# Decay attention and a snake MLP on one core: masks written directly in bf16, and the order of all engines written anew

## The chip, the core and the metric

The kernel runs on one NeuronCore of a Trainium2 chip. Its engines are TensorE (PE, its weight loads PEld), VectorE (DVE), ScalarE (ACT), GpSimd (POOL) and SyncE (SP); an issue queue is written with a q (SPq, POOLq). The metric is the device time of one execution in microseconds (us). A measurement is the median of several executions.

## What is computed

Causal attention with a decay per head, over 4 batches, 8 heads, 768 positions and head dimension 64, and behind it a two-layer MLP on the 3072 tokens of width 512 with 2048 hidden units:

```python
for b in range(nb):                      # blocks of 64 positions, in order
    intra = np.einsum('bhic,bhjc->bhij', qb, kb) * Dmask[None]      # lam**(i-j), i >= j
    intra = np.einsum('bhij,bhjd->bhid', intra, vb)
    inter = np.einsum('bhid,bhde->bhie', qb * lam_pow[None], kv_state)
    out[:, :, sl] = intra + inter
    kv_state = lam_block[None, :, None, None] * kv_state + np.einsum('bhsd,bhse->bhde', kb_dec, vb)
x = np.ascontiguousarray(attn_out.transpose(0, 2, 1, 3)).reshape(B * S, H * D)
h = x @ w_in
s = np.sin(alpha * h)
g = h + s * s / (alpha + 1e-09)
return (g @ w_out).astype(np.float32)
```

## The kernel before

**Attention.** The kernel takes blocks of 128 positions: 24 of them, six a batch. The decay is put into the operands: q is multiplied by lam to the position (L471 for the first four blocks, L481 for later ones), k by lam to minus the position (L488, L500). The factors `Lq`, `Lk`, `Lp` are Exp on ACT (L446 to L452) of `lnL`, a VectorE product (L444) of `E_f` and the logarithm of lam (L441); `E_f` is a GpSimd cast (L420) of three IOTA (L414, L416, L418). What remains of the decay mask is a mask of ones and zeros. v is only cast to bf16 (L494, L503). A block's q and k are transposed (on TensorE for the first eight blocks, L542, L569 and L519, by DMA later, L509) and copied out of PSUM as `qkT` (L547, L580, L552, L524). Then S, all scores of a block (L621), goes to PSUM; VectorE multiplies it by the mask and writes `Sm` in bf16 (L632); Z adds the block's k and v to the running state in PSUM bank 7 (L657, L665), which is copied out as `Zd` or `Zc` (L675, L681); and O adds Sm times v (L768 for the first four blocks, L725 later) and the state times q (L788, L703, L716). The result is cast to bf16 as `xT` (L748, L735), the transposed input of the MLP.

**MLP.** It takes six chunks of 512 tokens (four blocks). Stage A makes 16 products of 128 hidden units: L831 with 512 columns at once, L865 with two halves of 256. Each goes to one PSUM bank; ACT takes Sin of it (`t`, L841 or L875), ACT or GpSimd squares that (`u`, L845/L846 or L879/L880), and VectorE forms `gT` (L848, L883) from u and the bank, which is free again then. Stage B multiplies by w_out: directly for chunk 0 (L896); for the others by Strassen's scheme of seven products (L984), for which sums of weights (L939, into `ws`, `Ta` and `w`) and of tokens (L962, `Xs` and `gT`) are made on VectorE or GpSimd, and VectorE combines the results (L1024, L1030). Attention of later blocks stands between the products of earlier chunks.

**Loads.** SP issues the loads of q, k and v in its order; each waits until its ring buffer is free. The first 512 columns of w_in come in f32 as `ws` and are cast (L395). The other three blocks of w_in and the four of w_out come as DMAs that GpSimd issues (L326); they wait for the first v, and the loads of blocks 4 and 5 of q and behind it wait for the w_in block of columns 1024 to 1535 (the second of the three).

**The masks.** There are three: masks 0 and 1 for the first four blocks, whose positions are interleaved, mask 2 for all others. VectorE sets all three to one in f32 (`maskf`, L427), GpSimd clears what lies ahead of the diagonal (L431: two instructions of 64 rows each for masks 0 and 1, one of 128 rows for mask 2), and VectorE casts each to bf16 (L436).

**The order.** Each operation is recorded with an index, in program order (`op`). `ORDER` holds, for each engine, the list of the indices that it runs, in this order; where an operation may run on one of several engines, the list that holds it decides. A pair like `(31, 512)` in TensorE's list is filler: 31 products of the constant tile `idle` (a part of `Xs`) with 512 columns, whose result nobody reads (L1143). `_settle` walks the lists, and `emit` puts the waits in front of each instruction (L431's instructions on masks 0 and 1 wait for the GpSimd instruction ahead of them).

Of the kernel before, what the change touches and what calls it, by code (L numbers as in the profile page):

```python
# [8 lines left out]
F32 = mybir.dt.float32  # L9
# [26 lines left out]
class _Plan:  # L36
# [16 lines left out]
        ),  # L53
        "ACT": (
# [162 lines left out]
def bass_lightning_attn__then__act_snake_kernel(  # L217
# [41 lines left out]
    with es:  # L259

        def sb(name, shape, dt):
            return es.enter_context(nc.sbuf_tensor(name, shape, dt))
# [29 lines left out]
        mask = ring("mask", 3, [128, 128], BF16)  # L292
        maskf = sb("maskf", [128, 3, 128], F32)
# [21 lines left out]
        def _(_unused_eng):  # L315
# [4 lines left out]
            op = P.op  # L320
# [107 lines left out]
            for i in range(3):  # L428
                t, ks = (4, 2) if i < 2 else (2, 1)
# [828 lines left out]
```

## Time and profile before

| | |
|---|---|
| median of 3 runs | 212.16 us (211.62 to 213.02) |
| profiled execution | 212.84 us |
| its span, from the first to the last instruction | 211.0 us |
| busy share of the span | PE 95%, DVE 79%, ACT 72%, PEld 64%, POOL 61% |
| HBM read, written | 27.28 MB, 6.29 MB |

The profile is of one execution. The page gives busy time by engine, the timeline gives one row for each run of like instructions on an engine: start and length in us, engine, line, operation, what it writes and reads, count, and in brackets how long the engine had been idle and what ended that. The chain of waits follows the end of the program back, at each step to what released it. A busy TensorE includes matmuls that overlap: one of 512 columns shows as 379 ns, while they follow each other more closely.

### The profile page before, as it was taken

How to read it: one execution, taken by the hardware profiler on the slowest of the kernel's cores; microseconds unless marked ns; L12 is line 12 of the kernel's file. 1: busy time of each engine (PE TensorE's matmuls, PEld its weight loads, DVE VectorE, ACT ScalarE, POOL GpSimd, SP SyncE). 2: the span in 40 equal slices, each digit the busy share in tenths (PEclk: the TensorE clock that was granted, in tenths of full speed). 3: DMA queues.
4: the chain of work that ended last, by engine and by line, in shares of the span. 5: the costliest groups of instructions: out<-in, count | busy, mean ns of one | idle time of the engine just before them, and what ended most of it. 6: DMA issues, size and time to landing. Idle time of an engine off the chain costs nothing.

```text
span 211.0 us, 4818 instructions
## 1 busy us (share of the span) xinstructions
PE 201.1 (95%) x1927; PEld 135.5 (64%) x1950; DVE 167.5 (79%) x295; ACT 152.7 (72%) x279; POOL 127.9 (61%) x133
## 2 busy tenths in 40 slices
PE   6998899989999999999999999999999999999995
PEld 2476544546777787666566577666667666676994
DVE  1788467886779999989999988789886787587833
ACT  4448887837999999996777886976996667767100
POOL 5123476957698784955693653864995464923620
PEclk9999999999999999999999999999999999999999
DMA  4999999999969999997999998248000000500424
GB/s 135 313 314 224 211 225 196 252 198 254 260 120 180 226 201 249 228 241 190 209 224 197 236 204 234 42 109 243 3 0 0 3 0 0 199 3 0 168 71 163
DMA packets 83222, 34.40 MB, mean 163 GB/s; under 512 B 59632, under 2 KB 80384, under 8 KB 83200
## 3 DMA queue, kind: packets, MB, share of 16 engines
q1 hardware_dynamic: 78544, 29.24, 62.2%
q0 software_dynamic: 3696, 3.67, 10.8%
q10 hardware_dynamic: 960, 1.19, 1.9%
q8 instruction: 15, 0.25, 0.5%
q14 instruction: 7, 0.06, 0.1%
HBM read 27.28 MB, written 6.29 MB: 159 GB/s over the span
## 4 chain that ended last, share of the span: by engine, by line
PE 69%; DVE 16%; ACT 11%; issue 2%; ACTq 0%
PE bank L831 25%; PE bank L984 22%; PE bank L896 5%; PE bank L865 5%; PE bank L1143 5%; DVE gT L883 4%; ACT u L845 3%; DVE Sm L632 3%; ACT t L841 3%; DVE gT L848 3%; PE bank L621 2%; PE bank L725 2%; ACT Zd L675 1%; DVE Xs L962 1%; PE bank L657 1%
## 5 line engine op out<-in xcount | busy, mean ns | idle before, releaser
L831 PE MATMUL bank<-xT,w 128*128 128x512 bf16 x279 | 67.6, 379 | 2.8 <-issue 0.6
L848 DVE SCALAR_TENSOR_TENSOR gT<-u,rinv,bank 128x512 bf16<-128x512 bf16 x74 | 53.8, 742 | 17.6 <-ACT u L845 11.7
L841 ACT ACTIVATE t<-bank,alpha 128x512 bf16<-128x512 f32 x74 | 49.9, 683 | 21.4 <-PE bank L831 20.7
L831 PEld LDWEIGHTS bank<-xT,w 128*128 128x128 bf16 x296 | 27.6, 98 | 29.3 <-DVE gT L848 2.2
L962 POOL TENSOR_TENSOR gT<-gT 128x512 bf16<-128x512 bf16 x29 | 33.4, 1159 | 15.9 <-DVE Xs L962 7.6
L845 ACT ACTIVATE u<-t 128x512 bf16<-128x512 bf16 x62 | 38.2, 627 | 2.2 <-ACT t L841 0.6
L632 DVE TENSOR_TENSOR Sm<-bank,mask 128x1024 bf16<-128x1024 f32 x24 | 28.9, 1216 | 2.0 <-PE bank L657 1.8
L846 POOL TENSOR_TENSOR u<-t 128x512 bf16<-128x512 bf16 x12 | 12.4, 1039 | 26.2 <-ACT t L841 25.3
L962 POOL TENSOR_TENSOR Xs<-gT 128x512 bf16<-128x512 bf16 x17 | 19.3, 1154 | 4.7 <-DVE gT L848 4.7
L865 PE MATMUL bank<-xT,w 128*128 128x256 bf16 x176 | 21.7, 273 | 0.0
L883 DVE SCALAR_TENSOR_TENSOR gT<-u,rinv,bank 128x256 bf16<-128x256 bf16 x44 | 18.7, 474 | 3.4 <-POOL u L880 2.1
L984 PE MATMUL bank<-w,gT 128*128 128x256 bf16 (+1 forms) x168 | 19.9, 267 | 0.0
L984 PE MATMUL bank<-ws,gT 128*128 128x256 bf16 x160 | 19.9, 273 | 0.0
L875 ACT ACTIVATE t<-bank,alpha 128x256 bf16<-128x256 f32 x44 | 18.6, 474 | 1.5 <-PE bank L865 1.4
L984 PE MATMUL bank<-w,Xs 128*128 128x256 bf16 (+1 forms) x168 | 19.3, 268 | 0.0
L984 PEld LDWEIGHTS bank<-w,gT 128*128 128x128 bf16 x168 | 15.9, 98 | 4.3
L865 PEld LDWEIGHTS bank<-xT,w 128*128 128x128 bf16 x176 | 16.1, 98 | 3.2 <-ACT xT L735 0.4
L500 POOL TENSOR_TENSOR qk<-k,Lk 128x512 bf16<-128x512 f32 x16 | 17.1, 1074 | 1.3 <-DMA k<-in_k_dram 1.3
L984 PEld LDWEIGHTS bank<-w,Xs 128*128 128x128 bf16 x168 | 15.8, 98 | 3.2
L984 PEld LDWEIGHTS bank<-ws,gT 128*128 128x128 bf16 x160 | 15.5, 98 | 3.5
L481 POOL TENSOR_TENSOR qk<-q,Lq 128x512 bf16<-128x512 f32 x15 | 15.5, 1042 | 0.0
L896 PE MATMUL bank<-w,gT 128*128 128x512 bf16 x58 | 14.7, 379 | 0.3
(107 smaller groups left out, 275.3 us busy)
## 6 DMA issues: line engine op xcount, KB each, us to landing
q<-in_q_dram SPq DMA_DIRECT2D x12, 512.0 KB, 6.2
k<-in_k_dram SPq DMA_DIRECT2D x24, 256.0 KB, 5.1
v<-in_v_dram SPq DMA_DIRECT2D x24, 256.0 KB, 4.8
out_dram<-osb SPq DMA_DIRECT2D x18, 256.0 KB, 2.6
w<-in_moe_w_out_dram POOLq DMA_DIRECT2D x4, 512.0 KB, 10.8
w<-in_moe_w_in_dram POOLq DMA_DIRECT2D x3, 512.0 KB, 8.1
ws<-in_moe_w_in_dram SPq DMA_DIRECT2D x2, 512.0 KB, 6.3
out_dram<-osb ACTq DMA_DIRECT2D x8, 128.0 KB, 3.4
```

What stands on the lines that cost most here:

```text
L500: lambda e: e.tensor_tensor(qk2[:, j, H:2 * H, :], block32(k32, jl), lk, ALU.mult), 1.05,
L632: op("DVE", lambda e: e.tensor_tensor(Sm[js][:, :, :], banks[:, 512 * b0:512 * b0 + 1024].rearrange("p (c i) -> p c i", i=128), bass.AP(ma ...
L831: ins = e.matmul(ps[hb][:, c0:c1], w1[:, kc, 128 * m:128 * (m + 1)], xT[x][:, kc, c0:c1], start=(kc == 0 and c0 == lo), stop=(kc == NKC - ...
L841: op("ACT", lambda e: e.activation(t16[ju][:, w], ps[hb][:, w], ACTF.Sin, scale=alpha[:, m:m + 1]), 0.69 if hi - lo == TCH else 0.475, [ba ...
L845: lambda e: (e.activation(u16[ju][:, w], t16[ju][:, w], ACTF.Square) if e is nc.scalar else e.tensor_tensor(u16[ju][:, w], t16[ju][:, w], ...
L848: op("DVE", lambda e: e.scalar_tensor_tensor(out=gT[g][:, m, w], in0=u16[ju][:, w], scalar=rinv[:, m:m + 1], in1=ps[hb][:, w], op0=ALU.mul ...
L865: ins = e.matmul(ps[hb][:, 256 * i:256 * i + 256], w1[:, kc, 128 * (m + i):128 * (m + i + 1)], xT[x][:, kc, lo:lo + 256], start=(kc == 0 a ...
L875: op("ACT", lambda e, i=i: e.activation(t16[ju][:, 256 * i:256 * i + 256], ps[hb][:, 256 * i:256 * i + 256], ACTF.Sin, scale=alpha[:, m + ...
L883: op("DVE", lambda e, i=i: e.scalar_tensor_tensor(out=gT[g][:, m + i, lo:lo + 256], in0=u16[ju][:, 256 * i:256 * i + 256], scalar=rinv[:, ...
L896: ins = e.matmul(ps[ob][:, w], gT[g][:, m, 128 * s4:128 * (s4 + 1)], w2[:, m, w], start=(m == 0), stop=(m == NM - 1),)
L962: e.tensor_tensor(dst, in0, in1, alu), 0, rd, wr))
L984: ins = e.matmul(ps[ob][:, lo + d0:lo + d1], lhs, rhs[:, d0:d1], start=first and p == 0, stop=(p == NM // 2 - 1), skip_group_check=True)
```

## The change

The masks are set to one and cut directly in bf16: three VectorE memsets of 128 x 128 in place of one of 128 x 384 in f32, the same five GpSimd instructions on them, and no casts. There is one operation fewer, so that most indices in `ORDER` are smaller by one. `ORDER` itself is written anew for all five engines, and with it the filler.

```diff
     ORDER = {
         "PE": (
-            (31, 512), 59, 61, 39, 62, 57, 55, 53, (16, 128), 65, 75, 69, 70, 67, (14, 128), 73, 82, 78, 80, 87,
...
+            (64, 128), 58, (5, 512), 60, 54, (11, 128), 38, 56, 52, 61, 66, 64, (1, 128), 68, 69, 74, 77,
+            (2, 512), 72, 81, 79, 84, 86, 89, 90, 92, 123, 129, 139, 143, 135, 146, 150, 158, 162, 166, 174,
...
-        maskf = sb("maskf", [128, 3, 128], F32)
...
-            op("DVE", lambda e: e.memset(maskf[:, :, :], 1.0), 0.3, writes=[("maskf", i) for i in range(3)])
             for i in range(3):
+                op("DVE", lambda e, i=i: e.memset(mask[i][:, :], 1.0), 0.2, writes=[("mask", i)])
                 t, ks = (4, 2) if i < 2 else (2, 1)
                 for r in ((0, 64), (64, 128)) if i < 2 else ((0, 128),):
                     part = op("POOL", lambda e, i=i, r=r, t=t, ks=ks: e.affine_select(
-                        out=maskf[r[0]:r[1], i, :], in_=maskf[r[0]:r[1], i, :], pattern=[[1, t], [t, 128 // t]],
+                        out=mask[i][r[0]:r[1], :], in_=mask[i][r[0]:r[1], :], pattern=[[1, t], [t, 128 // t]],
                         compare_op=ALU.is_ge, fill=0.0, base=-i if i < 2 else 0, channel_multiplier=-ks), 0.3,
-                       [("maskf", i)], [("maskf", i)])
+                       [("mask", i)], [("mask", i)])
                     part.some = i < 2
-                op("DVE", lambda e, i=i: e.tensor_copy(mask[i][:, :], maskf[:, i, :]), 0.2, [("maskf", i)], [("mask", i)])
```

In the rows that follow, lines of the changed kernel are two or three smaller than those of the kernel before (L544 there is L547 here). VectorE, from the first scaling of q and k to the first product with a mask (`Sm`), before:

```order
L471 TENSOR_TENSOR qk2<-q32,Lq 128x2x256 x2
L488 TENSOR_TENSOR qk2<-k32,Lp 128x2x256
L471 TENSOR_TENSOR qk2<-q32,Lq 128x2x256
L494 COPY v2<-v32 128x2x256
L580 COPY qkT<-bank 128x512
L547 COPY qkT<-bank 128x2x256
L436 COPY mask_1<-maskf 128x128
L547 COPY qkT<-bank 128x2x256
L488 TENSOR_TENSOR qk2<-k32,Lp 128x2x256 x2
L436 COPY mask_0<-maskf 128x128
L632 TENSOR_TENSOR Sm_0<-bank,mask_0 128x1024
```

and now:

```order
L468 TENSOR_TENSOR qk2<-q32,Lq 128x2x256 x2
L485 TENSOR_TENSOR qk2<-k32,Lp 128x2x256
L468 TENSOR_TENSOR qk2<-q32,Lq 128x2x256 x2
L485 TENSOR_TENSOR qk2<-k32,Lp 128x2x256
L426 MEMSET mask_2 128x128
L544 COPY qkT<-bank 128x2x256
L577 COPY qkT<-bank 128x512 x2
L629 TENSOR_TENSOR Sm_1<-bank,mask_1 128x1024
```

The casts of masks 0 and 1 and of v have left this stretch, as have one k scaling (now on GpSimd) and one L547 copy (now on ACT); one L580 copy and the memset of mask 2 have come in.

ACT, from the copies of the state (`Zd`) of blocks 0 and 1 to the first Sin (`t16`), before:

```order
L675 COPY Zd_0<-bank 64x4x64
L675 COPY Zd_1<-bank 64x4x64 x2
L494 COPY v2<-v32 128x2x256
L395 COPY w1<-ws 128x4x256
L748 COPY xT_0<-bank 128x4x2x2x32
L675 COPY Zd_0<-bank 64x4x64 x2
L748 COPY xT_0<-bank 128x4x2x2x32
L748 COPY xT_0<-bank 128x2x2x2x32
L875 ACTIVATE t16_0<-bank,alpha 128x256 x2
```

and now:

```order
L672 COPY Zd_1<-bank 64x4x64
L491 COPY v2<-v32 128x2x256
L672 COPY Zd_1<-bank 64x4x64
L393 COPY w1<-ws 128x4x256
L672 COPY Zd_0<-bank 64x4x64 x2
L745 COPY xT_0<-bank 128x2x2x2x32
L393 COPY w1<-ws 128x4x256
L872 ACTIVATE t16_0<-bank,alpha 128x256 x2
```

Two xT copies have gone to VectorE; the second cast of w1 (L393), which VectorE did, has come to ACT. A v cast ahead of the first of these rows has gone to GpSimd; the v cast that is shown is that of another block (the last to be loaded, which GpSimd cast before).

TensorE, from the last products of the first four blocks (L788) into the MLP, before:

```order
L788 MATMUL bank<-qkT,Zd_0 128x128 x4
L865 MATMUL bank<-xT_0,w1 128x256 x8
L831 MATMUL bank<-xT_0,w1 128x512 x8
L657 MATMUL bank<-v2,qk2 128x128 x8
L865 MATMUL bank<-xT_0,w1 128x256 x8
L831 MATMUL bank<-xT_0,w1 128x512 x24
L896 MATMUL bank<-w2,gT_0 128x512 x4
```

and now:

```order
L785 MATMUL bank<-qkT,Zd_0 128x128 x4
L862 MATMUL bank<-xT_0,w1 128x256 x16
L828 MATMUL bank<-xT_0,w1 128x512 x4
L654 MATMUL bank<-v2,qk2 128x128 x8
L828 MATMUL bank<-xT_0,w1 128x512 x40
L893 MATMUL bank<-w2,gT_0 128x512 x4
```

The products are the same; the first use of w_out (L893) now stands behind three more units of stage A. On GpSimd the three DMAs of w_in stand together behind three v casts, and the first DMA of w_out behind the square of the second unit, where before two of w_in and the first of w_out stood ahead of the first square and the third of w_in behind it.

106 rows, old and new, of the table ORDER are left out of this document.

## The prediction, made before the changed kernel had run

> **What bounds the kernel now.** I read the page's first part, then the busy time in stretches, the timeline of the first 25 us, the tile view of the masks, the chain of waits and, last, the transfers. First the page and the stretches:
>
> ```profile
> PE 201.1 (95%) x1927; PEld 135.5 (64%) x1950; DVE 167.5 (79%) x295; ACT 152.7 (72%) x279; POOL 127.9 (61%) x133
> ```
>
> ```profile
> 10.00:20.00 10.00, 8.84 (x189) 6.89 (x187) 8.89 (x14) 5.89 (x13) 3.29 (x5) 1.00 1.19 278
> ...
> 46.00:208.50 162.50, 159.51 (x1537) 112.69 (x1555) 135.06 (x242) 120.86 (x220) 104.41 (x98) 1.00 0.66 144
> 22.18:46.00 23.82, 22.85 (x138) 11.55 (x138) 17.76 (x29) 18.76 (x33) 16.68 (x16) 1.00 1.17 219
> ```
>
> Behind the length of a stretch stand the busy times of PE, PEld, DVE, ACT and POOL, then the granted clock, the share of the DMA engines and GB/s. TensorE is the bound from 22.18 us on: it idles 0.97 us up to 46 us, and 2.99 us in the 162.5 behind. From its first L865 on, TensorE has the same products before and after the change, in nearly the same order. So the time is the start of that L865, plus a fixed body, plus idle time. The body can give 4 us at most; the rest lies in the 22 us ahead of it, where much of TensorE's busy time is filler (L1143).
>
> ```profile
> 1.66 9.56 PE L1143 MATMUL bank<-Xs 128*128 128x512 bf16 x31 [1.66 <-DVE Xs L421]
> ...
> 6.76 0.15 PEld L1143 LDWEIGHTS bank<-Xs 128*128 128x128 bf16 x1 [0.27 <-issue]
> ...
> 6.88 0.21 ACT L446 ACTIVATE Lq<-lnL 128x32 f32<-128x32 f32 x1
> ...
> 7.13 0.69 DVE L471 TENSOR_TENSOR qk<-q,Lq 128x512 bf16<-128x512 f32 x1 [0.68 <-ACT Lq L446]
> 7.17 3.55 PEld L1143 LDWEIGHTS bank<-Xs 128*128 128x128 bf16 x17 [0.26 <-issue]
> ...
> 15.27 4.62 DVE L632 TENSOR_TENSOR Sm<-bank,mask 128x1024 bf16<-128x1024 f32 x4
> ...
> 18.80 0.62 ACT L494 CAST v<-v 128x512 bf16<-128x512 f32 x1
> 19.32 1.04 ACT L395 CAST w<-ws 128x1024 bf16<-128x1024 f32 x1
> ...
> 20.39 0.73 ACT L748 CAST xT<-bank 128x512 bf16<-128x512 f32 x1
> ...
> 21.14 0.76 ACT L675 CAST Zd<-bank 64x256 bf16<-64x256 f32 x2
> ...
> 21.95 0.40 PE L788 MATMUL bank<-qkT,Zd 128*128 128x128 bf16 x4 [0.64 <-ACT Zd L675]
> ...
> 22.18 1.04 PE L865 MATMUL bank<-xT,w 128*128 128x256 bf16 x8
> ```
>
> Read this timeline upwards: L865 follows L788, which waits for two Zd copies on ACT, and these stand behind an xT copy, a cast of w1 and a cast of v. From 18.80 to 21.90 us ACT is the chain. Ahead of it VectorE is full from 7.13 us to the end of the four Sm products at 19.89.
>
> **The front, part by part.** *Start of the scaling.* At 7.13 VectorE has waited for Lq, the last of four Exp on ACT; they wait for lnL, and lnL for E_f.
>
> ```profile
> 5.52 0.20 ACT L443 ACTIVATE warm<-lnlam 128x1 f32<-128x1 f32 x1
> ...
> 5.75 0.29 POOL L420 CAST E_f<-E_i 128x128 f32<-128x128 int32 x1
> ...
> 6.15 0.29 DVE L444 TENSOR_TENSOR lnL<-E_f,lnlam 128x128 f32<-128x128 f32 x1 [4.14 <-POOL E_f L420]
> ```
>
> Two mask selects and a memset that stood ahead of E_f on GpSimd now stand behind it, and the first instruction there no longer waits for maskf. E_f comes before ACT is free at 5.72, so that ACT sets Lp (about 5.95) and Lq (6.35): 0.7 us earlier. The first two new memsets cost nothing, since VectorE waits there for E_f and then for Lp.
>
> *VectorE up to Sm.* Eight us lie between 7.13 and 15.27. A v cast, one k scaling, two mask casts and one L547 copy leave this stretch; one L580 copy and one memset come in. The first row is the tile view of the masks (minimum, median, maximum in ns), the others are the timeline:
>
> ```profile
> L436 DVE CAST mask<-maskf x3: 218/634/1756, 12.9 to 41.6; 128x128 bf16<-128x128 f32 x3
> ```
>
> ```profile
> 0.90 0.17 DVE L422 MEMSET identf<- 128x128 f32 x1 [0.90 <-PEq L1243]
> ...
> 10.88 0.42 DVE L494 CAST v<-v 128x512 bf16<-128x512 f32 x1
> ...
> 12.20 0.42 DVE L580 COPY qkT<-bank 128x512 bf16<-128x512 bf16 x1 [0.89 <-PE bank L569]
> ...
> 13.33 1.28 DVE L488 TENSOR_TENSOR qk<-k,Lp 128x512 bf16<-128x512 f32 x2
> ...
> 14.45 0.64 POOL L494 CAST v<-v 128x512 bf16<-128x512 f32 x1 [8.40 <-DMA v<-in_v_dram]
> 14.54 0.63 DVE L436 CAST mask<-maskf 128x128 bf16<-128x128 f32 x1
> ```
>
> Two casts of the front took 0.22 and 0.63, a copy counts as L580's 0.42, the memset as its nearest row, 0.17: 0.42 + 0.64 + 0.85 + 0.42 - 0.42 - 0.17 = 1.74 us. With the 0.7 Sm could start at 12.8. The wait of 0.89 for transposes shrinks too, since they are now issued one group at a time, not in a bunch behind 11 us of filler. I take Sm from 12.6 to 17.2, against 19.89. What can spoil it is the memset of mask 2, which runs while GpSimd scales a k block. The cast at 14.54 did: 0.63 instead of 0.22, ending with GpSimd's row above it. If the memset waits like that, Sm comes up to 0.8 us later; I leave this to the range. [...]
>
> *ACT up to L865.* After the change three xT copies (0.74 each) stand on VectorE behind Sm and are done by 19.4; the other v cast goes to GpSimd. ACT keeps, in this order, v, one Zd, w1, two Zd: 0.62 + 0.38 + 1.04 + 0.76 = 2.8. It starts behind other Zd copies near 16.0, when the last v block has long landed (14.45, the row above). So ACT is done at 18.8, and with 0.23 of L788 the first L865 starts at 19.1, where the second xT is there as well (18.7): 3.1 us earlier. A late Sm, a late transfer or a slower clock take up to 1.2 of it. The second cast of w1 now stands on ACT ahead of the first Sin; its 1.04 us leave the first units some 0.3 behind. I take 2.7 us, between 1.9 and 3.1.
>
> *The filler.* The granted clock reads 1.00 throughout, but the spacing of the loads tells the speed: 0.15 + 0.27 = 0.42 us for 512 columns ahead of 7.17, and 3.55 / 17 = 0.21 behind. Full speed came 5.5 us after the first product. At half speed 128 columns take 0.105, so 52 of the new 64 run slowly, the rest at 0.052, and they end at 7.8; if speed comes only behind them, at 8.4. The first scaled q block is there at 7.6. Five long and eleven short fillers (1.7 us) between the transposes lie in waits for VectorE. So the filler costs nothing in either case.
>
> **The third mask, mid-kernel.** From the chain of waits:
>
> ```profile
> 41.71 1.68 DVE mask L436
> 43.39 1.33 DVE gT L848 x2
> ...
> 44.76 0.40 PE bank L621 x8
> ```
>
> The cast of mask 2 (the 1756 ns) pushes two gT back, and L621 on TensorE, which needs their bank, with them. Now mask 2 is selected on GpSimd well ahead of its use. Gain 0.8 us; at least 0, if a copy of transposes is late in its place; at most 0.97, all idle time of that stretch.
>
> **What is given back.** The body now asks for its data 3 us sooner. From the page, the timeline and the transfers (the last column is us from issue to landing; 8.1 holds for the w_in issues at 16.24 and at 25.17):
>
> ```profile
> DMA  4999999999969999997999998248000000500424
> ```
>
> ```profile
> 16.24 0.76 POOL L326 DMA_DIRECT2D w<-in_moe_w_in_dram  x1
> 17.00 0.75 POOL L326 DMA_DIRECT2D w<-in_moe_w_out_dram  x1
> ...
> 22.88 3.89 SPq L326 DMA_DIRECT2D k<-in_k_dram  x1
> ...
> 25.17 0.80 POOL L326 DMA_DIRECT2D w<-in_moe_w_in_dram  x1
> ...
> 26.32 5.43 PE L831 MATMUL bank<-xT,w 128*128 128x512 bf16 x24
> ...
> 32.44 1.97 PE L831 MATMUL bank<-xT,w 128*128 128x512 bf16 x8
> ```
>
> ```profile
> k<-in_k_dram SPq DMA_DIRECT2D x1, 256.0 KB, 16.5
> ...
> w<-in_moe_w_in_dram POOLq DMA_DIRECT2D x1, 512.0 KB, 8.1
> ...
> w<-in_moe_w_out_dram POOLq DMA_DIRECT2D x1, 512.0 KB, 10.9
> ```
>
> The DMA engines are full for the first 100 us. The second and third weight block landed at 24.3 and 27.9, and the last w_in at 33.3, just as its product starts (half way through the row of 32.44). Now all three w_in are issued together behind the third v cast, near 14.5 us, and the first w_out fourth: 0.5 earlier than 27.9, and 3.6 more for one block, is 31.0. Its product comes, by the order, 16 x 0.109 + 44 x 0.22 + 0.3 = 11.7 us behind the first L865, at 30.8. Blocks 4 and 5 of q and k wait for the second w_in, some 2 us later than now, and one k block took 16.5 us beside the weights. Price: 0 (all just in time) to 2.5 us (landing as late as before). I take 1.0, since these rows show no slack.
>
> **The rest of the order.** Over a hundred instructions change engines behind that. TensorE's 2.99 us of idle time bound the gain, and as much again the loss, as its products and banks stay; I take 0. TensorE also gets 44 more instructions; what their fetch gives or costs is bounded by its waits for nothing visible, 0.6 us:
>
> ```profile
> PE bank L831 <- issue: 0.6, 4, 0.2
> ```
>
> **Sum.** The profiled execution took 212.84 us (span 211.0 and 1.84 around it), 0.68 above the median of 212.16. 212.84 - 2.7 - 0.8 + 1.0 = 210.3; on the median's footing 209.6 us, 1.2% faster. A measurement can tell about 1% from no change, so the borders are 210.0 and 214.3.
>
> **Rivals.** *The transfers eat the gain* (0.30). For it: full DMA engines and no slack at 33.3. Against it: part of what lands before 46 us (k, v and q of later blocks) may come after the weights. With 2.5 instead of 1.0: 211.1; with the front at 1.9 and the mask at 0.3 besides: 212.4. All within 1%.
>
> *The front gives all of it* (0.17): 3.1, the mask 0.97, nothing given back: 208.1, and 207.1 if the body loses one of its 2.99.
>
> *The clock falls back in the front* (0.09), the case on the other side. Against it: here the speed stays once it is reached. For it: the filler behind 10 us shrinks from 1.1 + 1.7 us to about 0.6. TensorE's 8.84 us from 10 to 20, less 2.8 of filler and 24 transposes of 0.055, hold some 5 of real products; at half speed they take 10, L865 starts near 23.0, and its first 5 us run slowly: 212.2 + 0.8 + 2.5 - 0.8 + 0.5 = 215.2. [...]
>
> *Masks in bf16 do nothing for the front*, their 0.85 us of casts being hidden: 210.4, inside the transfers' case.
>
> **Numbers.** Forecast 0.44 (208.7 to 210.5), transfers 0.30, full front 0.17, clock 0.09. Faster by over 1%: 0.17 and most of 0.44, 0.55; slower 0.09; within 1% 0.36. The range from 207.4 to 212.4 leaves out the clock and the far ends.
>
> **What would show it.** First L865 at 19.0 to 20.3 us; E_f before 5; Sm from about 12.6; no L436; loads of L1143 0.105 us apart, then 0.052; TensorE's idle time from L865 to 46 us below 2 us. The prediction is wrong if L865 starts behind 21 us, if products of 512 columns stand 0.42 us apart behind 13 us, or if the body's idle time passes 5 us.

## The result, and the profile after

| | before | after |
|---|---|---|
| median, measured side by side | 212.59 us (211.62 to 213.1) | 209.93 us (209.88 to 210.73) |
| ratio, with its 95% interval | | 0.9889 [0.9842, 0.9936] |
| profiled execution, its span | 212.84, 211.0 us | 209.95, 208.2 us |
| first product of stage A | 22.18 us | 19.04 us |

The changed kernel is 1.1% faster, 2.7 us; 209.6 us had been forecast. A ratio leaves out executions that are more than 1.5% longer than the shortest of their kernel, a median is over all, so that for some of the experiments below the two differ.

The page's busy times of the kernel after:

```profile
PE 200.0 (96%) x1972; PEld 136.8 (66%) x1972; DVE 168.5 (81%) x296; ACT 147.7 (71%) x270; POOL 132.4 (64%) x140
```

Rows of its timeline up to stage A, those between left out (start, length, engine, line, operation; in brackets the idle time before and what ended it):

```profile
1.66 5.60 PE L1140 MATMUL bank<-Xs 128*128 128x128 bf16 x64 [1.66 <-DVE Xs L419]
3.59 0.29 POOL L418 CAST E_f<-E_i 128x128 f32<-128x128 int32 x1
5.95 0.69 DVE L485 TENSOR_TENSOR qk<-k,Lp 128x512 bf16<-128x512 f32 x1 [1.41 <-ACT Lp L445]
7.43 0.40 PE L539 MATMUL bank<-ident,qk 128*128 128x128 bf16 x4 [0.17 <-DVE qk L468]
10.67 0.17 DVE L426 MEMSET mask<- 128x128 bf16 x1
10.74 1.04 POOL L485 TENSOR_TENSOR qk<-k,Lp 128x512 bf16<-128x512 f32 x1 [5.46 <-DMA k<-in_k_dram]
12.18 4.62 DVE L629 TENSOR_TENSOR Sm<-bank,mask 128x1024 bf16<-128x1024 f32 x4 [0.37 <-PE bank L618]
15.89 0.62 ACT L491 CAST v<-v 128x512 bf16<-128x512 f32 x1
18.00 0.76 ACT L672 CAST Zd<-bank 64x256 bf16<-64x256 f32 x2
18.81 0.40 PE L785 MATMUL bank<-qkT,Zd 128*128 128x128 bf16 x4 [0.34 <-ACT Zd L672]
19.04 1.91 PE L862 MATMUL bank<-xT,w 128*128 128x256 bf16 x16
```

Every event of the front stands earlier: the first scaling 1.18 us, the first Sm 3.09 (15.27 before), the first product of stage A 3.14. From Sm to that product it is 6.86 us, and it was 6.91: in time, what was gained lies ahead of Sm. The first scaling is now one of k (L485), which needs Lp alone. Both lists of VectorE's order in the section on the change start later than they say: a q and a k scaling (7.13 and 7.87 us) stand ahead of the first, this k scaling ahead of the second.

The weights and the third mask, from the timelines of GpSimd and TensorE:

```profile
15.09 2.43 POOL L324 DMA_DIRECT2D w<-in_moe_w_in_dram  x3
...
23.11 0.80 POOL L324 DMA_DIRECT2D w<-in_moe_w_out_dram  x1
```

```profile
22.30 8.81 PE L828 MATMUL bank<-xT,w 128*128 128x512 bf16 x40
30.94 1.03 PE L893 MATMUL bank<-w,gT 128*128 128x512 bf16 x4
...
39.66 0.40 PE L618 MATMUL bank<-qkT 64*128 64x128 bf16 x8
...
47.46 1.91 PE L862 MATMUL bank<-xT,w 128*128 128x256 bf16 x16
```

No row of these has a wait in brackets: all three blocks of w_in and the first of w_out are there in time, and the scores (L618), for which TensorE had waited near 44 us, wait no more. The products ahead of the row at 47.46 us are the same in both kernels; before, this row was

```profile
51.35 1.92 PE L865 MATMUL bank<-xT,w 128*128 128x256 bf16 x16
```

so that the kernel is 3.89 us ahead there, 3.14 of the front and 0.75 more. At the end it is 2.8 ahead (211.0 against 208.2). Behind 47 us 1.09 are given back. TensorE's two longest waits between 19 and 110 us (total, times, longest) are these:

```profile
PE bank L862 <- DVE gT L880: 1.0, 1, 1.0
PE bank L828 <- ACT kept L1018: 0.7, 1, 0.7
```

The second stands at 98 us. The first is at 65.21 us, and VectorE and GpSimd show this ahead of it:

```profile
60.55 1.76 DVE L880 SCALAR_TENSOR_TENSOR gT<-u,rinv,bank 128x256 bf16<-128x256 bf16 x4
62.24 2.13 DVE L936 TENSOR_TENSOR w<-w 128x1024 bf16<-128x1024 bf16 x2
64.29 0.86 DVE L880 SCALAR_TENSOR_TENSOR gT<-u,rinv,bank 128x256 bf16<-128x256 bf16 x2
```

```profile
62.22 1.60 POOL L497 TENSOR_TENSOR qk<-k,Lk 128x512 bf16<-128x512 f32 x1
```

Two weight sums stand ahead of the gT that frees TensorE's bank, and beside GpSimd's scaling they took 2.13 us, where one takes 0.69 elsewhere. In the kernel before, one of them was on GpSimd. Whether these waits are the whole of the 1.09 us isn't shown, since the kernel before has waits in this part, too.

### The profile page after: what moved, and what is told of

Read it like the earlier page. It is cut to its first block, busy times and chain, and to the rows that moved or that the text cites. A ratio compares the mean times of both kernels' runs of the same rounds, so it can differ in the third digit from the quotient of the medians.

```text
span 208.2 us, 4897 instructions
## 1 busy us (share of the span) xinstructions
PE 200.0 (96%) x1972; PEld 136.8 (66%) x1972; DVE 168.5 (81%) x296; ACT 147.7 (71%) x270; POOL 132.4 (64%) x140
## 4 chain that ended last, share of the span: by engine, by line
PE 79%; DVE 9%; ACT 4%; DMA 3%; SPq 2%; issue 1%; ACTq 1%; POOL 0%
PE bank L828 28%; PE bank L981 26%; PE bank L862 7%; PE bank L893 6%; PE bank L722 3%; PE bank L618 3%; DMA v<-in_v_dram 3%; SPq L324 2%; DVE gT L880 2%; DVE Sm L629 2%; DVE gT L845 2%; PE bank L700 1%; DVE w L936 1%; PE bank L654 1%; ACT Zd L672 1%; PE bank L662 1%
## 5 line engine op out<-in xcount | busy, mean ns | idle before, releaser
L828 PE MATMUL bank<-xT,w 128*128 128x512 bf16 x296 | 70.9, 380 | 1.0 <-ACT kept L1018 0.7
L959 POOL TENSOR_TENSOR gT<-gT 128x512 bf16<-128x512 bf16 x28 | 32.1, 1158 | 14.1 <-DVE Xs L959 8.9
L842 ACT ACTIVATE u<-t 128x512 bf16<-128x512 bf16 x57 | 35.2, 628 | 1.5
L843 POOL TENSOR_TENSOR u<-t 128x512 bf16<-128x512 bf16 x17 | 17.6, 1040 | 25.7 <-ACT t L838 25.7
L862 PE MATMUL bank<-xT,w 128*128 128x256 bf16 x176 | 21.6, 273 | 1.0 <-DVE gT L880 1.0
L959 POOL TENSOR_TENSOR Xs<-gT 128x512 bf16<-128x512 bf16 x19 | 21.8, 1162 | 0.3 <-DVE gT L845 0.3
L981 PE MATMUL bank<-ws,gT 128*128 128x256 bf16 x160 | 19.6, 273 | 0.0
L478 POOL TENSOR_TENSOR qk<-q,Lq 128x512 bf16<-128x512 f32 x17 | 18.2, 1077 | 2.0 <-DMA q<-in_q_dram 2.0
L862 PEld LDWEIGHTS bank<-xT,w 128*128 128x128 bf16 x176 | 16.3, 98 | 4.2 <-DVE gT L880 1.8
L893 PE MATMUL bank<-w,gT 128*128 128x512 bf16 x64 | 15.8, 380 | 0.0
```

Source lines behind the costliest of these rows:

```text
L478: lambda e, a=a: e.tensor_tensor(qk2[:, j:j + 2, 4 * a:4 * a + 4, :], q32[:, jq, 4 * a:4 * a + 4, :, :].rearrange("p h t d -> p t h d"), b ...
L828: ins = e.matmul(ps[hb][:, c0:c1], w1[:, kc, 128 * m:128 * (m + 1)], xT[x][:, kc, c0:c1], start=(kc == 0 and c0 == lo), stop=(kc == NKC - ...
L842: lambda e: (e.activation(u16[ju][:, w], t16[ju][:, w], ACTF.Square) if e is nc.scalar else e.tensor_tensor(u16[ju][:, w], t16[ju][:, w], ...
L862: ins = e.matmul(ps[hb][:, 256 * i:256 * i + 256], w1[:, kc, 128 * (m + i):128 * (m + i + 1)], xT[x][:, kc, lo:lo + 256], start=(kc == 0 a ...
L893: ins = e.matmul(ps[ob][:, w], gT[g][:, m, 128 * s4:128 * (s4 + 1)], w2[:, m, w], start=(m == 0), stop=(m == NM - 1),)
L959: e.tensor_tensor(dst, in0, in1, alu), 0, rd, wr))
```

## The experiments

This table of the profiles serves several of them (us; the columns are the first transposes and the first product of stage A on TensorE, and the first Sm on VectorE):

| kernel | transposes | Sm | stage A | Sm to stage A |
|---|---|---|---|---|
| before | 11.06 | 15.27 | 22.18 | 6.91 |
| masks_only | 10.16 | 13.81 | 21.29 | 7.48 |
| before_short_filler | 9.22 | 14.66 | 22.40 | 7.74 |
| after | 7.43 | 12.18 | 19.04 | 6.86 |
| front_only | 7.73 | 12.47 | 19.33 | 6.86 |
| until_47 | 7.91 | 12.65 | 19.51 | 6.86 |
| sum_later | 7.87 | 12.62 | 19.47 | 6.85 |
| order_only | 7.83 | 12.57 | 19.66 | 7.09 |
| vector_back | 7.45 | 14.06 | 21.02 | 6.96 |
| after_long_filler | 10.76 | 15.50 | 22.35 | 6.85 |

### The masks and the order, each alone

*masks_only*: the order of the kernel before, with the change's masks. The three casts (26, 23, 28) leave VectorE's list, two memsets come in, and all higher indices fall by one:

```diff
         "DVE": (
-            17, 16, 20, 33, 43,
+            17, 16, 20, 23, 26, 32, 42,
...
-            48, 63, 58, 26, 56, 49, 50, 23, 66, 68,
+            47, 62, 57, 55, 48, 49, 65, 67,
...
-            145, 182, 28, 194, 190,
+            144, 181, 193, 189,
```

> The order of the kernel before, on all engines, with the masks written in bf16 (three memsets where one stood, no casts). Theory 1, the casts lay on the path: the 1.76 us cast of mask 2 goes, so the 0.98 us stall of TensorE before the scores near 44 us goes (0.8 to 0.98 us), and the two casts of 0.22 and 0.63 us go from VectorE ahead of the first Sm, of which 0 to 0.85 us reach the first L862, since the ACT chain (cast of v, Zd, cast of w1, xT, Zd) stands behind it as before: 0.8 to 1.8 us faster than before. Rival, the casts filled waits and something else is late next: within 0.3 us of before.

Measured: 212.24 us, ratio 0.9985 [0.9959, 1.0011]. The stall before the scores is gone, and TensorE's waits between 24 and 48 us now read

```profile
PE bank L829 <- DMA w<-in_moe_w_in_dram: 0.4, 1, 0.4
PE bank L894 <- DMA w<-in_moe_w_out_dram: 0.3, 1, 0.3
```

From the first product of stage A (21.29 us) to a later row of 16 of them, at 58.01 us, it is 36.72 us; before it was 36.72 as well (22.18 to 58.90). What the mask no longer takes, the weights take. The first product of stage A stands 0.89 us earlier, but so do the first transposes behind the filler (10.16 against 11.06): the filler's weight loads stand 0.43 us apart up to 5.05 us and 0.21 from 5.41 on in this execution, and in that of the kernel before 0.43 up to 6.76 and 0.21 from 7.17 on. The rival was right, something else is late next.

*order_only*: the changed kernel's order, with f32 masks and casts, two ahead of the first uses and the third where the kernel before had it.

```diff
         "DVE": (
-            63, 62, 67, 65, 78,
+            64, 63, 68, 23, 66, 79,
...
-            181, 207, 193, 189,
+            182, 208, 28, 194, 190,
```

> The order of the changed kernel, on all engines, with f32 masks and casts: the casts of masks 1 and 0 stand on VectorE just ahead of the first uses, the cast of mask 2 where the kernel before had it. Theory 1: the front loses 0.3 to 0.85 us against the changed kernel (first L862 at 19.3 to 19.9 us) and the cast of mask 2 costs 0.2 to 1.0 us again near 40 us: 0.5 to 1.8 us slower than the changed kernel, 1 to 2.2 us faster than before. Rival: the order gives all of the gain, and this kernel is as fast as the changed one within 0.3 us.

Measured: ratio 0.9937 [0.9905, 0.9969]; the twelve executions lay between 210.68 and 215.02 us, seven of them at 214 us or more. In the front the casts cost 0.23 us (11.83 us from transposes to stage A, where four other kernels with this front have 11.60), and the filler starts 0.27 us later (1.93 against 1.66 us), behind the longer memset. The third cast cost far more, in the profile of one of the long executions:

```profile
37.45 4.19 POOL L938 TENSOR_TENSOR ws<-w 128x1024 bf16<-128x1024 bf16 x2
```

```profile
38.18 3.55 DVE L435 CAST mask<-maskf 128x128 bf16<-128x128 f32 x1
```

```profile
43.43 0.40 PE L620 MATMUL bank<-qkT 64*128 64x128 bf16 x8 [3.08 <-DVE qkT L523]
43.76 0.40 PE L518 MATMUL bank<-ident,qk 128*128 128x128 bf16 x4
44.21 3.02 PE L895 MATMUL bank<-w,gT 128*128 128x512 bf16 x7
```

A mask cast that took 0.22 us in the kernel before (12.87 us, GpSimd idle) lasted 3.55 here, to 41.73; the two weight sums on GpSimd ended at 41.64. TensorE idled 3.08 us for the copy behind it, and the eight products that follow (one record is missing) took 2.81 us, to 47.02, where eight of 512 columns take 1.73: the granted clock was 0.53 from 44.2 to 47 us. So the third cast cost little in the place that the old order gave it, and much in the new one, in this execution. The mean granted clock was 0.992 in six of the seven long executions and 0.999 to 1.000 in the five short ones; none of the five has a profile, so what the cast costs them isn't shown. By the ratio, which rests on these five, the kernel is 1.0 us slower than the changed one, as theory 1 has it, but the intervals of the two overlap.

### Where the gain sits: the order cut at three places

Each kernel has the changed kernel's lists up to a place in the program (with all that these operations depend on) and the remaining operations in the order, and on the engines, of the kernel before; bf16 masks in all. *front_only* is cut ahead of the first L862. TensorE's list there, against the changed kernel's:

```diff
-L862 MATMUL bank<-xT,w 128x256 x16
-L828 MATMUL bank<-xT,w 128x512 x4
+L863 MATMUL bank<-xT,w 128x256 x8
+L829 MATMUL bank<-xT,w 128x512 x8
 L655 MATMUL bank<-v,qk 128x128 x8
```

> The changed kernel's order up to the first L862 (filler, scaling, transposes, first four blocks, casts of w1), and the order of the kernel before in all that follows, the weight DMAs of GpSimd too; bf16 masks. Theory 1, the front is a gain by itself: first L862 at 19.0 us, 3.1 us earlier, and with the third mask ready the stall near 44 us is gone: 3 to 4 us faster than before, 208.6 to 209.6 us. Rival, the front needs the new order of the weight DMAs, since the old one brings the last block of w_in just in time at 33.3 us: 1 to 2.5 us of it are waited for between 25 and 46 us, 210 to 211.6 us.

Measured: 209.49 us, ratio 0.9845 [0.9812, 0.9878]. The front alone gives all of the gain, at 19.33 us for the first product. The row behind it:

```profile
21.24 1.67 PE L829 MATMUL bank<-xT,w 128*128 128x512 bf16 x7 [0.87 <-ACT w L394]
```

The units at the seam ask for the second cast of w1 too early. By then the weights were there: no wait for them follows. Behind the row that stands at 47.46 us in the changed kernel, this one needs 158.7 us (48.44 to 207.1), the kernel before 159.65, the changed one 160.7. (The profile is of this kernel's shortest execution, 0.5 us below its median.)

*until_22* moves the cut behind the first 20 products and the Z of block 3, so that the seam asks for nothing early:

```diff
-L863 MATMUL bank<-xT,w 128x256 x8
-L829 MATMUL bank<-xT,w 128x512 x8
+L863 MATMUL bank<-xT,w 128x256 x16
+L829 MATMUL bank<-xT,w 128x512 x4
 L655 MATMUL bank<-v,qk 128x128 x8
```

> The changed kernel's order up to its first 20 products of stage A and the Z of block 3, and the order of the kernel before behind that; bf16 masks. With the cut ahead of the first L862 TensorE lost 1.04 us near 20.2 us, waiting for the second cast of w1, as the order of the units behind the cut didn't fit the casts ahead of it. Theory 1, that was the only price of the cut: 1.0 us faster than that kernel, 2.2 to 2.6% faster than before (207.6 to 208.3 us), and 1 us or more faster than the changed kernel, whose body gives 1.1 us back. Rival, the body waits for the weights instead, 0.4 to 1 us near 30 and 45 us as with the masks alone: as fast as the cut ahead of the first L862.

Measured: 209.99 us, ratio 0.9888 [0.9857, 0.992]. The rival was right: with GpSimd's old order of the weight DMAs TensorE now waits

```profile
24.36 2.88 PE L829 MATMUL bank<-xT,w 128*128 128x512 bf16 x12 [0.81 <-DMA w<-in_moe_w_in_dram]
```

*until_47* is cut ahead of the row at 47.46 us, so that it has the new order of the weights. GpSimd's rows just behind the cut, against the changed kernel's:

```diff
 L936 TENSOR_TENSOR ws<-w 128x1024 x2
 L500 COPY v<-v 128x512
+L936 TENSOR_TENSOR ws<-w 128x1024
 L478 TENSOR_TENSOR qk<-q,Lq 128x2x256 x2
```

> The changed kernel's order up to the products at 47 us, where the trace shows it 3.9 us ahead, and the order of the kernel before behind that; bf16 masks. Theory 1, the 1.1 us that are given back at 63 to 65 us and 96 us come from the new order there (a weight sum on VectorE beside GpSimd, copies on ACT behind DMA issues): the 3.9 us are kept, 1.0 us faster than the changed kernel. Rival, they come from loads of k and v that are late whatever the order is, since TensorE is 3.9 us earlier: as slow as the changed kernel, within 0.4 us, with stalls of 0.5 to 1 us between 55 and 100 us.

Measured: 211.11 us, ratio 0.9912 [0.9876, 0.9948]. TensorE waits for no weights, but 0.4 us for an xT copy on ACT at 48.6 us, 0.5 for the `kept` copy on ACT and 0.4 for a copy of the state on VectorE. Theory 1 falls for this cut: from its row at 48.61 us on it needs as long as the changed kernel. But front_only, with all of the old body, is also early at this row and needs 2.0 us less. The profiles from this row (16 products of 256 columns) to the end, in us:

| kernel | order behind the row | row | to the end |
|---|---|---|---|
| before | old | 51.35 | 159.65 |
| front_only | old | 48.44 | 158.7 |
| until_22 | old | 49.20 | 159.0 |
| until_47 | old | 48.61 | 160.6 |
| after | new | 47.46 | 160.7 |
| sum_later | new, one sum moved | 47.92 | 160.8 |
| after_40 | new | 48.11 | 159.7 |
| after_long_filler | new | 51.49 | 159.5 |

So neither the new order alone nor an early TensorE alone loses the 1.1 us: the old order from the first product on loses nothing when it is early, the new one loses nothing when it is late, and after_40, the new order with a shorter first filler, loses nothing to speak of. The cause stays open.

### The filler: short with the old order, long with the new

```diff
         "PE": (
-            (31, 512), 59, 61, 39,
+            (64, 128), 59, 61, 39,
```

> The kernel before with one change: its first filler is 64 products of 128 columns (the changed kernel's) instead of 31 of 512. In the profiles so far the first L865 stands at a fixed distance behind the end of that filler: 11.12 us in the kernel before, 11.13 with its masks in bf16, 11.60 to 11.61 with the changed front. Theory 1, the filler's end sets the front: it ends at 7.3 to 7.9 us, and the first L865 starts at 18.5 to 19.2 us instead of 22.2. Rival, the prediction's steps: VectorE's stretch (full from 7.13 to 15.27 us but for a wait of 0.89) and the ACT chain set it, and the filler is nearly hidden: first L865 at 21.3 us or later. By theory 1 the whole gains 1 to 3 us, since TensorE would then wait for the third block of w_in, which landed at 33.3 us; by the rival 0 to 0.9 us.

Measured: 212.28 us, ratio 0.9984 [0.9957, 1.0011]. TensorE's rows:

```profile
1.66 6.41 PE L1143 MATMUL bank<-Xs 128*128 128x128 bf16 x64 [1.66 <-DVE Xs L421]
9.22 0.40 PE L542 MATMUL bank<-ident,qk 128*128 128x128 bf16 x4 [1.15 <-DVE qk L471]
...
12.36 1.90 PE L1143 MATMUL bank<-Xs 128*128 128x128 bf16 x16
...
22.40 1.04 PE L865 MATMUL bank<-xT,w 128*128 128x256 bf16 x8
```

The transposes don't follow the filler, they wait for VectorE's third scaling, and Sm comes only 0.61 us earlier than before. Theory 1 falls; the rival, the prediction's reading, stands. The filler at 12.36 us ran at half speed (16 in 1.90 us, where 16 took 1.06 in the kernel before): the granted clock was 0.72 from 10 to 16 us, which took back the rest. Of the ten executions four kept a mean granted clock of 1.00 and took 211.44 to 212.19 us, about 1 us less than the kernel before; the other six, at 0.992, took 212.26 to 213.1. So the short filler gains something where the clock holds, and the fall takes it. The opposite edit to the changed kernel:

```diff
         "PE": (
-            (64, 128), 58, (5, 512), 60, 54,
+            (31, 512), 58, (5, 512), 60, 54,
```

> The changed kernel with the first filler of the kernel before, 31 products of 512 columns. The short filler alone gave the kernel before nothing. Theory 1, the new order needs the short filler as well: the filler ends at 10.2 to 11.1 us, the first L862 comes 11.6 us behind it, at 21.8 to 22.7 us, and the whole front gain of 3.1 us is gone: 212 to 213 us, less if the body runs better with its loads ahead. Rival, with VectorE done earlier the row behind the filler gets shorter, since the transposed operands and the masks wait for nothing: 20.5 to 21.5 us.

Measured: 212.68 us, ratio 0.9996 [0.9968, 1.0024]; the first product at 22.35 us, 11.59 behind the transposes at 10.76. All of the gain is gone. Over all executions neither half shows a gain alone.

### The filler and the clock

```diff
         "PE": (
-            (64, 128), 58, (5, 512), 60, 54,
+            (40, 128), 58, (5, 512), 60, 54,
```

> The changed kernel with 40 instead of 64 products in its first filler. At half speed they end at 5.9 us, before the clock has risen in most profiles (5.3 to 7.1 us), and TensorE then waits until 7.4 us for the first scaled q. Theory 1, the clock rises at a moment of its own: the first L862 comes at 19.0 us, the earliest that the scaled q allows, 0 to 0.5 us earlier than in the changed kernel, whichever moment that is. Rival, the wait of 1.5 us puts the rise off: filler and transposes run at half speed beyond 7.4 us, first L862 at 20 us or later, 1 to 3 us slower than the changed kernel.

Measured: ten executions from 209.53 to 214.51 us, median 212.8, ratio 0.9923 [0.9874, 0.9973]. Three lie below 210.5 us, and the profile is of the shortest: the first product at 19.30 us, and full speed from the first transposes at 7.46 us on (the five products of 512 columns behind them in 1.24 us, as in the changed kernel). Seven lie at 212.5 us or more. So theory 1 holds for some executions and the rival's times for the others; none of these has a profile here. Six of the seven show a mean granted clock of 0.976 to 0.992, the three short ones 0.999 or 1.000, so most of them lose to a fall of the clock; where it fell stays open.

```diff
         "PE": (
-            (64, 128), 58, (5, 512), 60, 54, (11, 128), 38, 56, 52, 61, 66, 64, (1, 128), 68, 69, 74, 77,
-            (2, 512), 72, 81,
+            (64, 128), 58, 60, 54, 38, 56, 52, 61, 66, 64, 68, 69, 74, 77,
+            72, 81,
```

> The changed kernel without the filler between the transposes (five of 512 columns, eleven and one of 128, two of 512); the first 64 stay. Theory 1, it lies on the path as the first filler does: TensorE is 1.7 us less busy there, but the second half of q lands at 8.8 to 9.2 us and its scaling ends at 10.1 to 10.5, so that 0 to 0.5 us are gained in the front. Prediction's step: it costs nothing, 0 gain. Rival, it holds the clock up: without it products of 512 columns stand 0.42 us apart again behind 10 us, and the first L862 comes 1 us later or more.

Measured: 212.43 us, ratio 0.9979 [0.9942, 1.0015]. The first Sm comes at 11.96 us, 4.37 behind the transposes instead of 4.75, so that this filler costs 0.4 us at most. But the busy time in stretches (length, PE, PEld, DVE, ACT, POOL, then the granted clock) reads

```profile
16.00:18.00 2.00, 0.87 (x12) 0.52 (x10) 1.81 (x3) 1.93 (x4) 0.34 (x1) 1.00 1.22 247
18.00:20.00 2.00, 1.64 (x44) 1.44 (x45) 0.63 (x2) 0.90 (x4) 0.56 (x1) 0.89 1.24 209
20.00:23.00 3.00, 2.83 (x14) 1.96 (x13) 0.76 (x4) 1.92 (x5) 0.48 (x1) 0.50 1.24 208
```

and the first 16 products of stage A took 3.43 us instead of 1.91. The rival was right on the clock, though the fall comes near 19.6 us and not at 10, and the first product only 0.35 us later (19.39 us): without the filler between the transposes the granted clock fell to 0.50 in this profile. It doesn't in every execution: four of ten kept a mean of 1.000 and took 210.35 to 212.28 us.

### The steps of the front

*vector_back* puts a k scaling and a v cast back on VectorE:

```diff
         "DVE": (
-            41, 40, 48, 26, 55,
+            41, 40, 48, 49, 47, 26, 55,
...
         "POOL": (
-            29, 24, 25, 49, 46, 47, 51,
+            29, 24, 25, 46, 51,
```

> The changed kernel with the v cast and the k scaling that went to GpSimd put back on VectorE, ahead of the first Sm. The prediction's step: they lie on VectorE's stretch up to Sm, 0.42 + 0.61 = 1.03 us: Sm starts at 13.2 instead of 12.2 us and the first L862 at 19.8 to 20.1 us. Rival, TensorE's own row of transposes, filler and waits for ACT sets the front, from the end of the first filler to the first L862 in 11.6 us: Sm up to 1 us later, but the first L862 within 0.3 us of 11.6 us behind the filler's end. In time: 0.7 to 1 us slower than the changed kernel, or the same.

Measured: 214.66 us, ratio 1.0071 [1.0029, 1.0113]. VectorE's rows:

```profile
9.99 1.31 DVE L485 TENSOR_TENSOR qk<-k,Lp 128x512 bf16<-128x512 f32 x2
12.36 0.43 DVE L491 CAST v<-v 128x512 bf16<-128x512 f32 x1 [1.06 <-DMA v<-in_v_dram]
...
14.06 4.62 DVE L629 TENSOR_TENSOR Sm<-bank,mask 128x1024 bf16<-128x1024 f32 x4 [0.20 <-PE bank L618]
```

Sm stands 1.88 us later, 1.04 of work and 1.06 of waiting for v less 0.2 of a wait that is gone, and the first product 1.98 later, at 21.02. So VectorE has no slack ahead of Sm; at that place v hasn't landed either. The whole is far slower than the 0.7 to 1 us that were expected: 4.7 us by the medians. In the profiled execution (213.16 us) TensorE also waits 1.3 us for the `kept` copy and 1.1 us for w_out later on, and nine of the ten executions show a mean granted clock of 0.984 or less.

*act_back* gives ACT the chain of the kernel before:

```diff
         "ACT": (
-            82, 50, 83, 97, 87, 88, 94, 98, 125,
+            82, 50, 83, 98, 80, 87, 88, 91, 94, 125,
...
         "DVE": (
-            78, 73, 85, 80, 91, 93,
+            78, 73, 85, 97, 93,
```

> The changed kernel with ACT's row of the kernel before ahead of the first Sin: two xT copies back on ACT, one of them ahead of the last Zd copies, and the cast of the first half of w1 on VectorE. The prediction's step: the ACT chain sets the first L862, and a copy of 0.73 us in it puts L862 0.7 us off, to 19.7 to 19.9 us: 0.5 to 0.9 us slower than the changed kernel. Rival, the Zd copies wait for TensorE anyway: within 0.2 us.

Measured: 213.72 us, ratio 1.0037 [1.0008, 1.0066]. ACT's and TensorE's rows:

```profile
18.40 1.04 ACT L393 CAST w<-ws 128x1024 bf16<-128x1024 f32 x1 [1.42 <-DMA ws<-in_moe_w_in_dram]
19.47 0.73 ACT L745 CAST xT<-bank 128x512 bf16<-128x512 f32 x1
```

```profile
20.87 0.61 PE L785 MATMUL bank<-qkT,Zd 128*128 128x128 bf16 x4 [2.31 <-ACT Zd L672]
21.27 3.62 PE L862 MATMUL bank<-xT,w 128*128 128x256 bf16 x16
```

The first product is 2.23 us later: 0.73 for the copy, as expected, and 1.42 because the edit asked for the half of w1 that hadn't landed. And the granted clock fell here too, from within TensorE's wait of 2.31 us on:

```profile
18.00:20.00 2.00, 0.55 (x21) 0.29 (x10) 0.14 (x1) 1.57 (x2) 0.73 (x1) 0.96 1.22 202
20.00:26.00 6.00, 5.13 (x24) 3.30 (x24) 0.76 (x3) 3.82 (x10) 0.46 (x2) 0.50 1.18 199
26.00:28.00 2.00, 2.00 (x15) 0.90 (x14) 1.56 (x4) 0.97 (x2) 1.98 (x3) 0.84 1.08 296
```

### The give-back at 64 us

*sum_later*: one of the two weight sums ahead of the gT at 64.29 us is moved behind a copy of the state.

```diff
         "DVE": (
-            306, 335, 334, 355, 356,
+            306, 335, 355, 356,
...
-            425, 427, 412, 413,
+            425, 427, 334, 412, 413,
```

> The changed kernel with one weight sum on VectorE moved from 62 us to some 14 us later, behind a copy of the state at 75.6 us; its product comes at 89.5 us. In the changed kernel two such sums took 2.13 us together at 62.24 us beside GpSimd's scaling (1.60 us, where one usually takes 1.04), and TensorE waited 0.97 us for the gT behind them. Theory 1, VectorE's queue with these sums is the cause of what is given back at 64 us: the wait shrinks to 0.3 us or less and the whole gains 0.7 to 1.0 us against the changed kernel (208.9 to 209.3 us). Rival, VectorE is full from 58 to 76 us and TensorE loses the same later, or the late loads of v and k set it: within 0.3 us of the changed kernel.

Measured: 211.19 us, ratio 0.9923 [0.9891, 0.9955]. TensorE's wait at 64 us is gone, and there is another:

```profile
PE bank L862 <- DVE xT L732: 1.1, 1, 1.1
```

The sum took 1.57 us at its new place (75.63 us), and an xT copy stood behind it. Theory 1 falls, and the rival's mechanism was right: VectorE was busy 19.02 of the 20 us from 58 to 78 in the changed kernel, and what was put off there was waited for elsewhere. The kernel isn't within 0.3 us of the changed one, but 0.7 us slower by the ratio, with intervals that overlap.

## Why the prediction was right, and where it wasn't

**The front** (2.7 us forecast, the sum of its steps 3.1; measured 3.14, first product at 19.04 against 19.1). What vector_back and act_back put back on VectorE and ACT arrives at the first product one for one, so neither has slack. But that VectorE's row up to Sm sets the front, as the prediction read it, is shown only in part. These are rows of the chains of waits: the first of the kernel before, then two of before_short_filler, then three of the changed kernel.

```profile
1.66 9.56 PE bank L1143 x31
```

```profile
10.45 0.61 DVE qk L471
...
11.11 1.46 PE bank L542 x12
```

```profile
6.35 6.02 DMA v<-in_v_dram
...
12.42 0.62 POOL v L491
...
13.09 0.62 PE bank L654 x8
```

In the kernel before the chain runs through the filler to 11.22 us, then through transposes, ACT's copies and Z to ACT, not through Sm. With the short filler it runs through VectorE's scalings, to 11.06. In the changed kernel it runs through a load of v that landed at 12.37, GpSimd's cast of it, Z and ACT; in until_47 through the filler and the transposes. These paths end within a few tenths of each other (TensorE waits 0.30 us for that v cast, VectorE 0.37 for the scores ahead of Sm), so the product could come 3.14 us earlier only because the change moved all of them together; the prediction added up VectorE's and ACT's. That its 19.1 met 19.04 so closely is partly luck, since the load of v wasn't in the sum as a bound.

The steps one by one: the start of the scaling came 1.18 us earlier instead of 0.7, since the first scaling now needs Lp alone (the first of q came at 6.69, 0.44 earlier). The mask casts, half of the 1.74 us of that step, were worth 0.23 (order_only) in the new order, and no gain shows for them alone in the old one (masks_only). The memset of mask 2 ran in 0.17 us, so the 0.8 us that it might have cost weren't paid. But the row hardly tests whether a memset waits beside GpSimd's scaling, since it started 0.07 us ahead of it (10.67 against 10.74). ACT's chain from the v cast to the Zd copies is 2.87 us long where it was 3.10: its gain is small, it mostly starts earlier.

**The filler** was priced at nothing, because it would end at 7.8 to 8.4 us where the data come at 7.6. In this execution it ended ahead of the data. In others the transposes came up to 7.91 us, and each tenth went into the first product (11.60 us behind in four profiles). The step missed that the old filler, ending at 11.22 us, hid the VectorE gain (after_long_filler: 22.35), as VectorE's scalings, ending at 11.06, hid the shorter filler (before_short_filler: Sm only 0.61 us earlier, and a fall of the clock behind it). The filler between the transposes was called free as well; it costs 0.4 us at most.

**The third mask** (0.8 us): 0.75 us was gained between the front and 47 us, but the mechanism is half the story. Alone the mask gave nothing, as the weights were due just behind it. The price was right because the weights were moved as well.

**What is given back** (1.0 us, to the weights at 31 us): wrong in place and cause. The three DMAs of w_in in a row did keep up: no wait to 47 us. The first product of w_out came at 30.94, as worked out (30.8), and its weights were there. The prediction took the landing times of the old order as a measure of the new one's. until_22 shows what the old order of the DMAs costs an early front: 0.81 us at 24.36.

**The rest of the order** (0, with 2.99 us either way): it gave back 1.09 us. The longest waits, at 65 and 98 us, are for VectorE and ACT, but an early TensorE alone isn't the cause, as front_only shows; what is stays open. So the forecast's 1.0 stands in the sum for a loss that it put elsewhere: two errors that cancel, which is luck. The 0.6 us that bounded the price of the instruction fetch were TensorE's waits for nothing visible; the list of the changed kernel's waits has none, so no run shows that a fetch cost anything. In its trace no matmul is missing (1972 for 1972 weight loads, where the trace before has 1927 for 1950), so those waits may have been gaps that missing records left.

**The clock** (0.09, 215.2 us): it didn't fall back in the changed kernel. What the rival feared with less filler is shown by after_no_inner_filler: without the filler between the transposes TensorE was busy 0.87 of the 2 us from 16 to 18 and the clock fell to 0.50 near 19.6; the mean clock lay at 0.974 to 0.992 in six of ten executions, and the whole is 2.5 us slower by the medians. How thin the work has to be for a fall, and for how long, isn't shown.

Front_only, the new front with the old body, is the best of all kernels by its ratio, 0.9845 against 0.9889; the intervals overlap, so it isn't shown to be faster.

## What to carry to other kernels

When two resources both end just ahead of a join (here the filler at 11.22 us and VectorE's scalings at 11.06), removing either alone gives little: price them together, and test with each half alone. Read the chain of waits for each kernel before calling one engine's full row the path. An early front is worth what the next supplier can follow, in until_22 the weights, in sum_later VectorE: each gain can show the next queue that has no room. A cast on VectorE that reads f32 and stands beside long GpSimd work should be taken out of the path even if it measures 0.2 us elsewhere: a mask cast of 128 x 128 took 0.22 us with GpSimd idle, 0.63 and 1.76 beside its work in the kernel before, and 3.55 beside two of its weight sums in order_only.

## What the runs showed of the hardware

The same 64 products of 128 columns, begun at 1.66 us, took 5.60 us in the changed kernel's profile and 6.41 in that of before_short_filler. The granted clock reads 1.00 over the first ten us of the kernel before, though the filler's weight loads stand 0.43 us apart there up to 6.76 us and 0.21 from 7.17 on; for later falls it shows 0.50 (from 20 to 23 us in after_no_inner_filler, from 20 to 26 in act_back).

Taken as time at 0.50, the falls of four profiles have one length or twice that: 3.4 us in after_no_inner_filler (0.89 over two us and 0.50 over three: 0.44 + 3.0), 3.4 in before_short_filler (0.72 over six), 3.4 in order_only (0.53 over 2.8 and 0.80 over two: 2.6 + 0.8), and twice as much, 6.8, in act_back (0.96 over two, 0.50 over six and 0.84 over two: 0.16 + 6.0 + 0.64). The mean granted clocks of single executions fit whole pieces as well: they stand, within 0.002, at 1.000, 0.992, 0.984, 0.976 and 0.968. A step of 0.008 of some 211 us is 1.7 us, half of 3.4.

In after_no_inner_filler the clock fell with no single wait behind the first transposes longer than 1.02 us, in a stretch in which TensorE was busy 0.87 of 2 us. In vector_back TensorE waited 2.56 us ahead of 13.59 and was busy 0.41 of the 2 us from 12 to 14, and the clock read 1.00 from 10 to 16 us and 1.000 in the mean. So a long wait wasn't needed for a fall, and one thin stretch didn't always bring it; what does isn't shown.
